# Probabilities transposed by a transfer of 16-bit halves, and a second layer two slices behind the first

## The chip, the core and the metric

The kernel runs on one core of a Trainium2 chip. A core has a matrix engine (TensorE, PE in the profile, with its weight loads as PEld), a vector engine (VectorE, DVE), a scalar engine (ScalarE, ACT), GpSimd (POOL) and SyncE (SP), which here only issues transfers. Each engine works through its own queue in order, and semaphores tie the queues together. Sixteen DMA engines move data between the chip's main memory (HBM) and the on-chip memory (SBUF), and within SBUF. TensorE writes to PSUM, eight banks of 128 x 512 floats.

The metric is the device time of one execution in microseconds: the median of three runs of the kernel before is 1006.57 us (1006.5 to 1007.86).

## The reference

Attention with a sliding window, with a few global tokens, followed by a dense two-layer network. Cut to what matters:

```python
# B = H = 8, Sl = 512 local and Sg = 32 global tokens, D = 64, window = 32
k_all, v_all = concat([k_g, k_l]), concat([v_g, v_l])
out_g = softmax(scale * q_g @ k_all.T) @ v_all
s_ll  = where(|i - j| <= window, scale * q_l @ k_l.T, -1e9)
out_l = softmax(concat([scale * q_l @ k_g.T, s_ll])) @ concat([v_g, v_l])
x = concat([out_g, out_l]) as [4608 tokens, 512]
h = x @ w_in                      # 512 -> 2048
out = (h * sigmoid(h)) @ w_out    # 2048 -> 512, float32
```

## The kernel before

**Attention in steps.** The local attention is cut into 64 steps (`steps`, numbered k): one step is a batch entry, a block of 128 queries and four of the eight heads. A step has two units i = 0, 1, and a unit has two heads u = 0, 1. For one head 128 queries meet W = 224 keys (128 + 2 x 32 local ones and 32 global ones). A step goes through these stages:

- `st_load`, `st_vload`: SP issues the loads of queries and keys (`raw`) and of values (`vraw`).
- `st_scores` (L352): 8 score products into the two PSUM banks "s".
- `st_soft`: per unit, `st_max` (L364, DVE: mask, scale and row minimum into the buffer `probs`), `st_exp` (L375, ACT), `st_norm` (L381, L383, DVE) and `st_scale` (ACT at L391 for u = 0, DVE at L389 for u = 1). There are two buffers `probs`, one for each unit.
- `st_move` (L397): SP copies the finished probabilities, 128 x 512 floats, from SBUF to SBUF into a buffer `rr` of the type float32r.
- `st_turn` (L427): TensorE turns them, four 128 x 128 transposes for each unit, into the "s" banks.
- `st_turned` (L439 on DVE, L441 on ACT): a copy from PSUM into `pt`, of which there are four.
- `st_with` (L453 to L456): POOL adds the global queries' columns to `pt`.
- `st_values` (L469): 16 products of `pt` with the values, into bank "x".
- `st_x` (L482 on ACT, L486 on DVE): the result as an upper part `xh` and a remainder `xl`, which are the network's input.

**Network in slices.** The tokens are cut into 12 blocks n of 2 or 3 tiles of 128 tokens, the hidden layer into 16 slices f of 128. Each float32 product is made of three float32r products (upper x upper, remainder x upper, upper x remainder). `first_layer(n, f)` is 12 products at L635 into one of two PSUM banks "h", then `g_tanh` (L642, ACT), `g_silu` (L646, DVE), `g_upper` (L652, ACT: `gh`) and `g_lower` (L658, DVE: `gl`). `second_layer(n, f)` is 9 products at L665 to L667. Before, the second layer runs one slice behind the first (`pend`). There are two buffers `gh` and one `gl`.

**What sets the order.** The start of the program, up to step 8 and the first block of tokens, is written out word by word (`START`). After that, the loop over blocks and slices hands out the stages of attention between the slices' products: each stage has a place on a scale of "step times" (`put`, `at(k)`, two units from one step to the next), and `fill` and `advance` release it when the share of the block's products that is done has come so far. In `group(k)` stand, for TensorE in this order, the transposes of step k - 1 (`turns`), the values of step k - 2 and the scores of step k. TensorE's order is the program's order; the order of the other engines is made by the scheduler of the compiler's tile layer, except where a dependency pins it. Loads have offsets of their own (`LOADS`). Global queries have their own chain (`g_scores` to `g_turned`), which the change leaves as it is.

Of the kernel before, what the change touches and what calls it, by code (L numbers as in the profile page):

```python
# [13 lines left out]
U32 = mybir.dt.uint32  # L14
AF = mybir.ActivationFunctionType
# [26 lines left out]
PARTS = 6  # L42
QK = P + W
# [37 lines left out]

FIRST = 0.6
APART, EARLY = 6, 0.1
LOADS = dict(load=-2.6, vload=0.3)
# [6 lines left out]
def attention_moe_kernel(ctx: ExitStack, tc: tile.TileContext, qk0_in, qk_in, v_in, gqk, wts, out):  # L91
# [33 lines left out]
    id32 = work.tile([P, P], F32R, tag="rr", bufs=2, name="id32").bitcast(F32)  # L125
# [30 lines left out]
    for t in probs:  # L156
        nc.gpsimd.memset(t[:, :, W:], 0.0)
    pgs = [const.tile([P, SKV], F32, name=f"pg{i}") for i in range(2)]
# [73 lines left out]
    def did(what, *needs):  # L232
        for need in needs:
            assert need in order_done, (what, need)
        order_done.add(what)

# [74 lines left out]
    def st_load(k):  # L311
        n = min(2, ND - 2 * k)
        of = qk0_in[2 * k : 2 * k + n].rearrange("i p n -> p i n")
        if k < WHOLE:

            if k % 4 < 2:
                raw = two.tile([P, 2 * (QW + W)], F32, tag="xh", name=f"raw{k}")
            else:
                raw = scratch(7 - k, F32, f"raw{k}")[:, : 2 * (QW + W)]
            nc.sync.dma_start(out=raw.rearrange("p (i n) -> p i n", i=2), in_=of)  # L320
            tiles["raw", k] = raw
            return
# [12 lines left out]
        tiles["raw", k] = raw  # L335
# [58 lines left out]
    def st_move(k, i):  # L394
        n = 2 * k + i
        rr = work.tile([P, 4 * P], F32R, tag="rr", bufs=2, name=f"rr{n}")
        nc.sync.dma_start(out=rr.bitcast(F32), in_=tiles["p", n])  # L397
# [12 lines left out]
    def st_turn(k, i):  # L410
# [11 lines left out]
        for m in range(4):  # L422
            sl = slice(m * P, (m + 1) * P)
            if k <= KF:
                nc.tensor.transpose(t[:, sl], p[:, sl], ident.bitcast(F32))  # L425
            else:
                nc.tensor.transpose(t[:, sl].bitcast(F32R), p[:, sl], ident)  # L427
# [44 lines left out]
    def st_x(k, rest=False):  # L472
# [8 lines left out]
        if not rest:  # L481
            nc.scalar.copy(out=xh[:, prs, sl], in_=src)  # L482
        if not rest and k >= AHEAD:
            return
        if rest:
            nc.vector.tensor_tensor(out=xl[:, prs, sl], in0=src, in1=xh[:, prs, sl].bitcast(F32), op=ALU.subtract)  # L486
            add_global(b, c, q2, gsrc)
        tiles.pop(("o", k))
# [70 lines left out]
    def put_last(n):  # L559

        places = [(two, "o", DM), (two, "o", DM), (raws, "vraw", DM // 2), (raws, "raw", DM // 2)]
        sb = [pool.tile([P, w], F32, tag=tag, name=f"o{n}_{i}") for i, (pool, tag, w) in enumerate(places)]
# [17 lines left out]
    plain_g = [two.tile([P, 3 * P], F32, tag="gh", name=f"g_first{t}") for t in range(2)]  # L580
# [57 lines left out]

    def g_tanh(n, f):
# [9 lines left out]
    def g_upper(n, f):  # L649
        nt = SIZES[n] * P  # L650
        gs[n, f] = [two.tile([P, 3 * P], F32R, tag="gh", name=f"gh{n}_{f}")]
        nc.scalar.copy(out=gs[n, f][0][:, :nt], in_=gs["t"][:, :nt])  # L652

    def g_lower(n, f):
        nt = SIZES[n] * P
        gs[n, f].append(two.tile([P, 3 * P], F32R, tag="gl", bufs=1, name=f"gl{n}_{f}"))
# [36 lines left out]
    traced, behind = nc.cur_bb.bb.instructions, {}  # L693
    pinned = mybir.DependencyInfo(mybir.DependencyClass.NoSync, mybir.DependencyReason.DATA)
# [25 lines left out]
    def turns(k):  # L720
        for i in range(2):
            st_turn(k, i)
        for i in range(2):
            st_turned(k, i)
            st_with(k, i)

    def group(k):

        if KF + APART < k <= len(steps):
            turns(k - 1)  # L730
        if k - 2 >= KF:
            st_values(k - 2)
            st_x(k - 2)
            st_x(k - 2, True)
        if k < len(steps):
# [15 lines left out]
    for k in range(KF + 1, len(steps) + 2):  # L751
        if k <= KF + APART:
# [35 lines left out]
    def fill(part):  # L788
# [3 lines left out]
        total = NF * SIZES[n] + (NF - 1) * SIZES[n] + SIZES[n - 1]  # L792
# [25 lines left out]
    pend = 0, PARTS - 1  # L818
    for n in range(1, len(SIZES)):
        for f in range(NF):  # L820
# [7 lines left out]
            second_layer(*pend)  # L828
            pend = n, f
    second_layer(*pend)  # L830
# [69 lines left out]
```

## Time and profile before

| what | value |
|---|---|
| median of the runs | 1006.57 us |
| the profiled execution | 1005.61 us |
| its span, first to last instruction | 1003.8 us |
| granted TensorE clock | 0.999 |
| L427 transposes | x440, in the trace from 108.6 to 905.0 us |
| L439 and L441, copies of the turned probabilities out of PSUM | 691 ns x63 and 583 ns x65 |
| POOL busy | 76.8 us, 8% of the span |
| moved by DMA | 110.15 MB, 110 GB/s mean |

A span is what lies between the first and the last instruction; the execution's own time is 1.8 us longer. Busy time of TensorE is no measure of its work by itself, because its products are pipelined and each is shown with its whole latency: consecutive products of 384 columns start 0.17 us apart and are each shown as 0.33 us long. What one costs is the distance from its start to the next one's.

### The profile page before, as it was taken

How to read it: one execution, taken by the hardware profiler on the slowest of the kernel's cores; microseconds unless marked ns; L12 is line 12 of the kernel's file. 1: busy time of each engine (PE TensorE's matmuls, PEld its weight loads, DVE VectorE, ACT ScalarE, POOL GpSimd, SP SyncE). 2: the span in 40 equal slices, each digit the busy share in tenths (PEclk: the TensorE clock that was granted, in tenths of full speed). 3: DMA queues.
4: the chain of work that ended last, by engine and by line, in shares of the span. 5: the costliest groups of instructions: out<-in, count | busy, mean ns of one | idle time of the engine just before them, and what ended most of it. 6: DMA issues, size and time to landing. Idle time of an engine off the chain costs nothing.

```text
span 1003.8 us, 17665 instructions
## 1 busy us (share of the span) xinstructions
PE 994.9 (99%) x6266; PEld 859.9 (86%) x6268; DVE 490.9 (49%) x1626; ACT 501.1 (50%) x1339; POOL 76.8 (8%) x234
## 2 busy tenths in 40 slices
PE   9999999999999999999999999999999999999998
PEld 5677887888888888888888888888888888888997
DVE  7887656444454445443445444544454444433222
ACT  7688676543554445453454444545444444432322
POOL 1033062000000000000000000000000000000000
PEclk9999999999999999999999999999999999999999
DMA  9973335322433224231142333324323231200001
GB/s 347 387 247 111 120 122 182 114 76 70 145 117 94 100 92 140 70 125 47 51 144 92 104 107 98 108 91 136 92 86 132 93 92 59 98 32 1 32 1 32
DMA packets 83880, 110.15 MB, mean 110 GB/s; under 512 B 7632, under 2 KB 55504, under 8 KB 83792
## 3 DMA queue, kind: packets, MB, share of 16 engines
q1 hardware_dynamic: 83456, 108.56, 32.8%
q8 instruction: 50, 0.82, 0.3%
q10 hardware_dynamic: 336, 0.46, 0.1%
q14 instruction: 38, 0.31, 0.1%
HBM read 67.37 MB, written 8.91 MB: 76 GB/s over the span
## 4 chain that ended last, share of the span: by engine, by line
PE 96%; DMA 1%; ACT 1%; DVE 1%; issue 1%; POOL 0%; POOLq 0%; ACTq 0%; DVEq 0%
PE h L635 36%; PE out L665 13%; PE out L666 12%; PE out L667 12%; PE o L469 7%; PE s L352 6%; PE t L427 3%; PE out L605 2%; PE gs L256 2%; PE h L589 2%; PE t L425 1%; PE gt L296 0%; PE idle L681 0%; DMA rr<-probs 0%; DMA raw<-in_qk_dram 0%
## 5 line engine op out<-in xcount | busy, mean ns | idle before, releaser
L635 PE MATMUL h<-xh,w_hi 128*128 128x384 f32 (+1 forms) x704 | 235.1, 334 | 0.0
L635 PE MATMUL h<-xh,w_lo 128*128 128x384 f32 (+1 forms) x704 | 233.9, 332 | 0.6 <-DMA w_lo<-w_lo 0.6
L635 PE MATMUL h<-xl,w_hi 128*128 128x384 f32 (+1 forms) x704 | 233.0, 331 | 0.0
L642 ACT ACTIVATE t<-h 128x384 f32<-128x384 f32 (+1 forms) x182 | 86.8, 477 | 272.9 <-PE h L635 271.0
L665 PE MATMUL out<-w_hi,gh 128*128 128x512 f32 x521 | 209.3, 402 | 0.0
L666 PE MATMUL out<-w_lo,gh 128*128 128x512 f32 x521 | 205.6, 395 | 0.0
L667 PE MATMUL out<-w_hi,gl 128*128 128x512 f32 x521 | 205.5, 394 | 0.0
L646 DVE SCALAR_TENSOR_TENSOR t<-t,h 128x384 f32<-128x384 f32 (+1 forms) x182 | 97.4, 535 | 209.9 <-ACT t L642 209.8
L658 DVE TENSOR_TENSOR gl<-t,gh 128x384 fp32r<-128x384 f32 (+1 forms) x182 | 100.1, 550 | 127.9 <-PE out L667 119.6
L635 PEld LDWEIGHTS h<-xh,w_hi 128*128 128x128 f32 x704 | 132.4, 188 | 10.6 <-issue 3.6
L635 PEld LDWEIGHTS h<-xl,w_hi 128*128 128x128 f32 x704 | 132.3, 188 | 6.7
L375 ACT ACTIVATE probs<-probs,st 128x224 f32<-128x224 f32 x236 | 111.5, 474 | 51.0 <-DVE st L364 51.0
L635 PEld LDWEIGHTS h<-xh,w_lo 128*128 128x128 f32 x704 | 132.2, 188 | 0.8 <-DMA w_lo<-w_lo 0.8
L652 ACT CAST gh<-t 128x384 fp32r<-128x384 f32 (+1 forms) x182 | 90.8, 499 | 76.4 <-DVE t L646 76.2
L665 PEld LDWEIGHTS out<-w_hi,gh 128*128 128x128 f32 x521 | 97.8, 188 | 29.7 <-issue 14.5
L667 PEld LDWEIGHTS out<-w_hi,gl 128*128 128x128 f32 x521 | 97.7, 188 | 21.9 <-DVE gl L658 0.5
L666 PEld LDWEIGHTS out<-w_lo,gh 128*128 128x128 f32 x521 | 97.9, 188 | 14.5
L453 POOL COPY pt<-pgt 128x64 f32<-128x64 f32 x120 | 29.5, 254 | 760.7 <-PE o L469 423.5
L364 DVE CUSTOM_DVE_ANT_0 probs<-s,mask 128x224 f32<-128x224 f32 x236 | 78.2, 387 | 4.8 <-PE s L352 4.8
L469 PE MATMUL o<-pt,vraw 128*64 128x160 f32 (+1 forms) x1024 | 78.2, 295 | 0.1
L439 DVE COPY pt<-t 128x512 f32<-128x512 f32 x63 | 43.4, 691 | 62.4 <-PE t L427 60.1
L469 PEld LDWEIGHTS o<-pt,vraw 128*64 128x64 f32 x1024 | 61.8, 136 | 6.5 <-issue 0.7
(104 smaller groups left out, 949.9 us busy)
## 6 DMA issues: line engine op xcount, KB each, us to landing
rr<-probs SPq DMA_DIRECT2D x110, 256.0 KB, 2.4
vraw<-in_v_dram SPq DMA_DIRECT2D x64, 256.0 KB, 2.7
raw_w<-in_wts_dram SPq DMA_DIRECT2D x32, 512.0 KB, 7.3
raw<-in_qk_dram SPq DMA_DIRECT2D x57, 224.0 KB, 2.8
graw<-in_gqk_dram SPq DMA_DIRECT2D x32, 304.0 KB, 3.3
out_dram<-o SPq DMA_DIRECT2D x30, 256.0 KB, 2.1
raw<-in_qk_dram SPq DMA_DIRECT2D x114, 64.0 KB, 2.4
pgr<-pg SPq DMA_DIRECT2D x12, 272.0 KB, 2.5
```

What stands on the lines that cost most here:

```text
L352: nc.tensor.matmul(s[u][:, i * W : (i + 1) * W], raw[rows, q : q + P], raw[rows, key : key + W], start=True, stop=True)
L364: nc.vector.tensor_tensor_reduce(out=p[:, u, :W], in0=s[u][:, i * W : (i + 1) * W], in1=mask_of[c], scale=-SCALE, scalar=3.0e38, op0=ALU.a ...
L375: nc.scalar.activation(p[:, u, :W], p[:, u, :W], AF.Exp, bias=st[:, m : m + 1], scale=-1.0, accum_out=st[:, 4 + m : 5 + m])
L469: nc.tensor.matmul(o[D * u : D * (u + 1), i * wide : i * wide + m], vraw[:, i, a, u, :], pts[i][:, u, a, :m], start=(a == 0), stop=(a == 1))
L635: nc.tensor.matmul(hs[n, f][:, :nt], wt, x, start=(i == 0), stop=(i == 3 * NCC - 1))
L642: nc.scalar.activation(t[:, :nt], hs[n, f][:, :nt], AF.Tanh, scale=0.5)
L646: nc.vector.scalar_tensor_tensor(out=t[:, :nt], in0=t[:, :nt], scalar=1.0, in1=hs.pop((n, f))[:, :nt], op0=ALU.add, op1=ALU.mult)
L652: nc.scalar.copy(out=gs[n, f][0][:, :nt], in_=gs["t"][:, :nt])
L658: nc.vector.tensor_tensor(out=gl[:, :nt], in0=gs["t"][:, :nt], in1=gh[:, :nt].bitcast(F32), op=ALU.subtract)
L665: nc.tensor.matmul(o, gh[:, sl], wh, start=(n > 0 and f == 0), stop=False)
L666: nc.tensor.matmul(o, gh[:, sl], wl, start=False, stop=False)
L667: nc.tensor.matmul(o, gl[:, sl], wh, start=False, stop=(f == (NF if n else PARTS) - 1))
```

## The change

From step 15 on (`TURNS = 15`) TensorE no longer transposes the local probabilities: 49 of the 64 steps. Instead:

- `st_split` (after's L408, DVE): the float32 words of a unit's probabilities are taken as pairs of 16-bit halves, and sorted into a plane of low halves and a plane of high halves (128 x 896 16-bit values, `planes`, one for each unit).
- L410: SP issues a transposing transfer of the planes, eight blocks of 128 x 128 16-bit values (256 KB), which lands in the buffer `probs` that the words came from.
- `st_join` (after's L417, ACT): a copy of 128 x 1024 16-bit values weaves the halves together again, into `pt`.

`st_move` goes for all steps; steps 9 to 14 are still turned by TensorE, straight from `probs` as float32. In `group(k)` the joins of step k - 1 now stand behind the values of step k - 2; `pt` has two buffers instead of four, and `raw` one instead of two from step 9 on, with its load asked for later. From the third block of tokens on (`LAG = 2`) the second layer runs two slices behind the first; `gh` and `gl` each have a ring of three places, made of buffers that are no longer used otherwise (`pt2`, `pt3`, `raw0`), and `g_upper` and `g_lower` are written out behind the second layer of the slice two before.

```diff
+LAG = 2
+
+TURNS = 15
...
-APART, EARLY = 6, 0.1
-LOADS = dict(load=-2.6, vload=0.3)
+EARLY = 0.1
+LOADS = dict(load=-1.9, vload=0.3)
...
+    planes = [const.tile([P, 2, 2, 2 * P], U16, name=f"planes{i}") for i in range(2)]
...
-        raw = raws.tile([P, 2 * QK], F32, tag="raw", name=f"raw{k}")
+        raw = raws.tile([P, 2 * QK], F32, tag=f"raw{k % 2 if k < KF else int(k > KF)}", bufs=1, name=f"raw{k}")
...
-    def st_move(k, i):
+
+    def st_split(k, i):
         n = 2 * k + i
-        rr = work.tile([P, 4 * P], F32R, tag="rr", bufs=2, name=f"rr{n}")
-        nc.sync.dma_start(out=rr.bitcast(F32), in_=tiles["p", n])
-        tiles["p", n] = rr
+        p = p_of(k, i)[:, :, :W].bitcast(U16).rearrange("p u (j h) -> p h u j", h=2)
+        nc.vector.tensor_copy(out=planes[i][:, :, :, :W], in_=p)
+        tiles["turned", n] = p_of(k, i).rearrange("p u j -> p (u j)").bitcast(U16).rearrange("p (g q) -> p g q", q=P)
+        nc.sync.dma_start_transpose(out=tiles["turned", n], in_=planes[i].rearrange("p h u j -> p (h u j)"))
+
+    def st_join(k, i):
+        _, b, c, q2 = steps[k]
+        n = 2 * k + i
+        did(("last", b, q2) if (c, i) == (NC - 1, 1) else ("step", n), ("turn", b, q2))
+        pt = pt_of(n).rearrange("p u a q -> p (u a) q").bitcast(U16)[:, :, : 2 * P].rearrange("p m (q h) -> p h m q", h=2)
+        nc.scalar.copy(out=pt, in_=tiles.pop(("turned", n)).rearrange("p (h m) q -> p h m q", h=2))
+        tc.add_manual_dep(traced[-1], state["evicted"], pinned, reason="join")
...
-            if k >= KF:
-                st_move(k, i)
+            if k >= TURNS:
+                st_split(k, i)
...
-            if k <= KF:
-                nc.tensor.transpose(t[:, sl], p[:, sl], ident.bitcast(F32))
-            else:
-                nc.tensor.transpose(t[:, sl].bitcast(F32R), p[:, sl], ident)
+            nc.tensor.transpose(t[:, sl], p[:, sl], ident.bitcast(F32))
...
-            tiles["pt", n] = work.tile([P, 2, 2, P + SG], F32, tag="pt", bufs=4, name=f"pt{n}")
+            tag = f"pt{n % (4 if n < 2 * TURNS else 2)}"
+            tiles["pt", n] = work.tile([P, 2, 2, P + SG], F32, tag=tag, name=f"pt{n}")
...
+    upper = [(two, "gh0"), (work, "pt2"), (two, "gh1")]
+    lower = [(work, "pt3"), (raws, "raw0"), (two, "gl")]
...
-        for i in range(2):
+        for i in range(2 if k < TURNS else 0):
             st_turn(k, i)
         for i in range(2):
-            st_turned(k, i)
+            (st_turned if k < TURNS else st_join)(k, i)
             st_with(k, i)
...
-        if KF + APART < k <= len(steps):
-            turns(k - 1)
         if k - 2 >= KF:
             st_values(k - 2)
             st_x(k - 2)
             st_x(k - 2, True)
+        if TURNS < k <= len(steps):
+            turns(k - 1)
...
-        for part in (g_tanh, g_silu, g_upper, g_lower):
+        for part in (g_tanh, g_silu) + (g_upper, g_lower) * (n < LAG):
             part(n, f)
...
-            second_layer(*pend)
-            pend = n, f
-    second_layer(*pend)
+            pend.append((n, f))
+            while len(pend) > (1 if n < LAG else 2):
+                second_layer(*pend.pop(0))
+            if n >= LAG:
+
+                for part, name in ((g_upper, "evicted"), (g_lower, "added")):
+                    part(n, f)
+                    if name in state:
+                        tc.add_manual_dep(traced[-1], state.pop(name), pinned, reason=name)
+    for slice_ in pend:
+        second_layer(*slice_)
```

How this stands in the queues is shown at the group of step 32, in block n = 4 of the tokens. TensorE's queue before: the last product of the slice h4_12, then the transposes of step 31 out of `rr`, the values of step 30 (`o30`), the scores of step 32 and the second layer of slice 11.

```order
L635 MATMUL h4_12_4678<-xh_4_3211,w_lo12_1860 128x384
L427 MATMUL t31_0_4698<-ident_88,rr62_4590 128x128 x4
L427 MATMUL t31_1_4699<-ident_88,rr63_4600 128x128 x4
L469 MATMUL o30_4718<-pt60_4545,vraw30_4468 64x160 x4
L469 MATMUL o30_4718<-pt61_4550,vraw30_4468 64x160 x4
L352 MATMUL s32_0_4730<-raw32_4525 128x224
L352 MATMUL s32_1_4731<-raw32_4525 128x224
L352 MATMUL s32_0_4730<-raw32_4525 128x224
L352 MATMUL s32_1_4731<-raw32_4525 128x224
L665 MATMUL out4_0_4086<-w_hi11_1819,gh4_11_4661 128x512
```

The same place in TensorE's queue with the change (all line numbers are after's):

```order
L656 MATMUL h4_12_4485<-xh_4_3086,w_lo12_1844 128x384
L487 MATMUL o30_4501<-pt60_4360,vraw30_4285 64x160 x4
L487 MATMUL o30_4501<-pt61_4365,vraw30_4285 64x160 x4
L362 MATMUL s32_0_4523<-raw32_4408 128x224
L362 MATMUL s32_1_4524<-raw32_4408 128x224
L362 MATMUL s32_0_4523<-raw32_4408 128x224
L362 MATMUL s32_1_4524<-raw32_4408 128x224
L694 MATMUL out4_0_4011<-w_hi10_1769,gh4_10_4452 128x512
```

The eight transposes are gone, the rest keeps its order, and the second layer that follows is that of slice 10 where it was that of slice 11.

ACT's queue at the same place before: tanh and upper part of slice 12 (`t4_12`, `gh4_12`) around the copy of a turned unit, the eviction `xh` of step 30, the exponentials and the scalings of step 32, tanh of slice 13.

```order
L642 ACTIVATE t4_12_4691<-h4_12_4678 128x384
L441 COPY pt62_4708<-t31_0_4698 128x4x128
L652 CAST gh4_12_4694<-t4_12_4691 128x384
L482 CAST xh_5_4123<-o30_4718 128x2x128
L375 ACTIVATE probs0_116,st32_4736<-probs0_116,st32_4736 128x224
L375 ACTIVATE probs1_117,st32_4736<-probs1_117,st32_4736 128x224
L375 ACTIVATE probs0_116,st32_4736<-probs0_116,st32_4736 128x224
L375 ACTIVATE probs1_117,st32_4736<-probs1_117,st32_4736 128x224
L391 ACTIVATE probs0_116<-probs0_116,st32_4736 128x224
L391 ACTIVATE probs1_117<-probs1_117,st32_4736 128x224
L642 ACTIVATE t4_13_4783<-h4_13_4770 128x384
```

With the change:

```order
L671 ACTIVATE t4_12_4498<-h4_12_4485 128x384
L500 CAST xh_5_3938<-o30_4501 128x2x128
L417 COPY pt62_4513<-probs0_116 128x2x4x128
L417 COPY pt63_4518<-probs1_117 128x2x4x128
L681 CAST gh4_12_4567<-t4_12_4498 128x384
L385 ACTIVATE probs0_116,st32_4529<-probs0_116,st32_4529 128x224 x2
L385 ACTIVATE probs1_117,st32_4529<-probs1_117,st32_4529 128x224 x2
L401 ACTIVATE probs0_116<-probs0_116,st32_4529 128x224
L401 ACTIVATE probs1_117<-probs1_117,st32_4529 128x224
L671 ACTIVATE t4_13_4584<-h4_13_4571 128x384
```

Both joins of step 31 stand between the eviction of step 30 and everything that ACT does for step 32; the upper part of slice 12 has moved behind them. On DVE the two splits (L408) stand behind both scalings of the step and ahead of the `g_silu` of slice 13.

SP's queue around step 31 with the change: the loads of the next step's queries and keys (`raw32`) and a move of the global chain (`pgr`) stand ahead of the transfers of step 31, the values of step 32 behind them.

```order
L350 DMA vraw31_4441<-in_v_dram 128x2x256
L337 DMA raw32_4408<-in_qk0_dram 64x2x128 x2
L338 DMA raw32_4408<-in_qk0_dram 128x2x224
L293 DMA pgr4_0_4412<-pg0_130 128x544
L410 DMA_TRANSPOSE probs0_116<-planes0_126 128x8x128
L410 DMA_TRANSPOSE probs1_117<-planes1_127 128x8x128
L293 DMA pgr4_1_4553<-pg1_131 128x544
L350 DMA vraw32_4562<-in_v_dram 128x2x256
```

The two transfers stand where the two moves into `rr` (L397) stood; before, the load of step 33 (`raw33`) stood ahead of the moves of step 31, so the load has come one step nearer to its use.

More of the change, by code (lines that the diff above doesn't have):

```diff
@@ L14 @@
 U32 = mybir.dt.uint32
+U16 = mybir.dt.uint16
 AF = mybir.ActivationFunctionType
@@ L124, in attention_moe_kernel @@
     nc.vector.memset(acc, 0.0)
-    id32 = work.tile([P, P], F32R, tag="rr", bufs=2, name="id32").bitcast(F32)
+    id32 = work.tile([P, P], F32, tag="pt0", name="id32")
     make_identity(nc, id32)
@@ L157, in attention_moe_kernel @@
         nc.gpsimd.memset(t[:, :, W:], 0.0)
+    planes = [const.tile([P, 2, 2, 2 * P], U16, name=f"planes{i}") for i in range(2)]
+    for t in planes:
+        nc.gpsimd.memset(t[:, :, :, W:], 0)
     pgs = [const.tile([P, SKV], F32, name=f"pg{i}") for i in range(2)]
@@ L235, in did @@
         order_done.add(what)
+    traced = nc.cur_bb.bb.instructions
+    pinned = mybir.DependencyInfo(mybir.DependencyClass.NoSync, mybir.DependencyReason.DATA)
     state = {}
@@ L482, in st_x @@
             nc.scalar.copy(out=xh[:, prs, sl], in_=src)
+            state["evicted"] = traced[-1].name
         if not rest and k >= AHEAD:
@@ L487, in st_x @@
             add_global(b, c, q2, gsrc)
+            state["added"] = traced[-1].name
         tiles.pop(("o", k))
@@ L559, in put_last @@
     def put_last(n):
-        places = [(two, "o", DM), (two, "o", DM), (raws, "vraw", DM // 2), (raws, "raw", DM // 2)]
-        sb = [pool.tile([P, w], F32, tag=tag, name=f"o{n}_{i}") for i, (pool, tag, w) in enumerate(places)]
+        places = [(two, "o", DM), (two, "o", DM), (raws, "vraw", DM // 2), (raws, "raw1", DM // 2)]
+        sb = [pool.tile([P, w], F32, tag=tag, bufs=1 if tag == "raw1" else 2, name=f"o{n}_{i}")
+              for i, (pool, tag, w) in enumerate(places)]
         src = outs[n][:2] + [outs[n][2][:, : DM // 2], outs[n][2][:, DM // 2 :]]
@@ L579, in attention_moe_kernel @@
     plain_h, plain_t = {}, two.tile([P, 3 * P], F32, tag="t", bufs=1, name="t_first")
-    plain_g = [two.tile([P, 3 * P], F32, tag="gh", name=f"g_first{t}") for t in range(2)]
+    plain_g = [two.tile([P, 3 * P], F32, tag=f"gh{t}", bufs=1, name=f"g_first{t}") for t in range(2)]
     def one(t, f):
@@ L636, in layer_products, with place @@
                 i += 1
+    upper = [(two, "gh0"), (work, "pt2"), (two, "gh1")]
+    lower = [(work, "pt3"), (raws, "raw0"), (two, "gl")]
+    def place(ring, short, n, f, name):
+        pool, tag = ring[((n - LAG) * NF + f) % 3] if n >= LAG else short[f % len(short)]
+        return pool.tile([P, 3 * P], F32R, tag=tag, bufs=1, name=f"{name}{n}_{f}")
     def g_tanh(n, f):
@@ L650, in g_upper @@
         nt = SIZES[n] * P
-        gs[n, f] = [two.tile([P, 3 * P], F32R, tag="gh", name=f"gh{n}_{f}")]
+        gs[n, f] = [place(upper, upper[::2], n, f, "gh")]
         nc.scalar.copy(out=gs[n, f][0][:, :nt], in_=gs["t"][:, :nt])
@@ L655, in g_lower @@
         nt = SIZES[n] * P
-        gs[n, f].append(two.tile([P, 3 * P], F32R, tag="gl", bufs=1, name=f"gl{n}_{f}"))
+        gs[n, f].append(place(lower, lower[2:], n, f, "gl"))
         gh, gl = gs[n, f]
@@ L692, in attention_moe_kernel @@
             does[name + letter] = partial(does[name], engine=engine)
-    traced, behind = nc.cur_bb.bb.instructions, {}
-    pinned = mybir.DependencyInfo(mybir.DependencyClass.NoSync, mybir.DependencyReason.DATA)
+    behind = {}
     for word in START.split():
@@ L751, in attention_moe_kernel @@
     for k in range(KF + 1, len(steps) + 2):
-        if k <= KF + APART:
+        if k <= TURNS:
             put(at(k) - (EARLY if k > KF + 1 else 0.4), turns, k - 1)
@@ L791, in fill @@
         n = now[0]
-        total = NF * SIZES[n] + (NF - 1) * SIZES[n] + SIZES[n - 1]
+        now_, then = (1 if m < LAG else 2 for m in (n, n - 1))
+        total = (2 * NF - now_) * SIZES[n] + then * SIZES[n - 1]
         if n + 1 < len(SIZES):
@@ L816, in second_layer @@
             put_out(n)
-    pend = 0, PARTS - 1
+    pend = [(0, PARTS - 1)]
     for n in range(1, len(SIZES)):
```

## The prediction

> **What bounds the kernel now.** First the page: span, busy times, and the chain of work that ended last.
>
> ```profile
> span 1003.8 us, 17665 instructions
> ...
> PE 994.9 (99%) x6266; PEld 859.9 (86%) x6268; DVE 490.9 (49%) x1626; ACT 501.1 (50%) x1339; POOL 76.8 (8%) x234
> ...
> PE 96%; DMA 1%; ACT 1%; DVE 1%; issue 1%; POOL 0%; POOLq 0%; ACTq 0%; DVEq 0%
> ```
>
> TensorE is busy for 99% of the span and carries 96% of the chain. Since its products overlap, the busy time alone proves little, so the second view is the windows, for the stretch in which all steps from 9 on are turned:
>
> ```profile
> 120.00:910.00 790.00, 789.24 (x4985) 692.56 (x4984) 373.95 (x1276) 385.26 (x1041) 52.55 (x178) 1.00 0.31 99
> ```
>
> Of 790.00 us TensorE shows work in 789.24, at the full clock (1.00), while DVE has 374 and ACT 385. Nothing that TensorE waits for is left to win there: **the time is the sum of what TensorE is given to do**. So the third view is its timeline, where a piece of work costs the distance from its start to the start of what follows.
>
> ```profile
> 514.20 0.39 PE L667 MATMUL out<-w_hi,gl 128*128 128x512 f32 x1
> 514.42 0.79 PE L427 MATMUL t<-ident,rr 128*128 128x128 f32 x8
> 515.15 1.20 PE L469 MATMUL o<-pt,vraw 128*64 128x160 f32 x16
> 516.28 1.03 PE L352 MATMUL s<-raw 64*128 64x224 f32 x8
> ```
>
> At 514.42 the eight transposes of a step take the place at which the next product would have started (514.20 + 0.23), and the values start at 515.15. That is **0.73 us a step**, not the 0.79 us shown nor the 243 ns of a single one. The same distance at other places:
>
> ```profile
> 162.08 0.80 PE L427 MATMUL t<-ident,rr 128*128 128x128 f32 x8
> 162.81 1.20 PE L469 MATMUL o<-pt,vraw 128*64 128x160 f32 x16
> ...
> 177.23 0.80 PE L427 MATMUL t<-ident,rr 128*128 128x128 f32 x8
> 177.96 1.31 PE L469 MATMUL o<-pt,vraw 128*64 128x160 f32 x16
> ...
> 190.39 0.80 PE L427 MATMUL t<-ident,rr 128*128 128x128 f32 x8
> 191.12 1.31 PE L469 MATMUL o<-pt,vraw 128*64 128x160 f32 x16
> ```
>
> 0.73 each time. The last view of this part is that of the line, for the number of steps and their distance:
>
> ```profile
> L427 PE MATMUL t<-ident,rr x440: 222/247/283, 108.8 to 905.0; 128*128 128x128 f32 x147
> ```
>
> 440 transposes are 55 steps (9 to 63), spread over 796 us: one step in 14.7 us.
>
> **What leaves TensorE.** Steps 15 to 63, 49 of them, lose their eight transposes: 49 x 0.73 = **35.8 us**, all on the path, because TensorE has no gaps there that could swallow it. What follows the transposes, the values, then follows a product as the transposes did, so no change-over is added. Steps 9 to 14 keep theirs, but in float32. What that costs is shown by step 8:
>
> ```profile
> 98.37 1.04 PE L425 MATMUL t<-ident,probs 128*128 128x128 f32 x8
> 99.16 0.47 PE L665 MATMUL out<-w_hi,gh 128*128 128x512 f32 x1
> ```
>
> 0.79 us for eight (98.37 to 99.16) against 0.73: 6 x 0.06 = 0.4 us back. Sum on TensorE: -35.4 us.
>
> **What is added, and what hides it.** Two splits on DVE, two transfers on SP, two joins on ACT for each of 49 steps; one copy on DVE and one on ACT go. The trace shows neither operation, so I bound them by rows of copies.
>
> ```profile
> L439 DVE COPY pt<-t 128x512 f32<-128x512 f32 x63 | 43.4, 691 | 62.4 <-PE t L427 60.1 <-PE t L425 1.3 <-POOL pt L453 0.2
> L389 DVE TENSOR_SCALAR probs<-probs,st 128x224 f32<-128x224 f32 x116 | 39.4, 340 | 1.5
> L646 DVE SCALAR_TENSOR_TENSOR t<-t,h 128x384 f32<-128x384 f32 x160 | 88.2, 552 | 198.7 <-ACT t L642 198.7
> L441 ACT COPY pt<-t 128x512 f32<-128x512 f32 x65 | 37.9, 583 | 15.3 <-PE t L427 12.7 <-PE t L425 1.6
> L652 ACT CAST gh<-t 128x384 fp32r<-128x384 f32 x160 | 81.9, 512 | 72.6 <-DVE t L646 72.4
> L486 DVE TENSOR_TENSOR xl<-o,xh 128x256 fp32r<-128x256 f32 x60 | 25.5, 425 | 42.4 <-ACT xh L482 42.3
> L482 ACT CAST xh<-o 128x256 fp32r<-128x256 f32 x60 | 22.3, 371 | 37.7 <-PE o L469 37.7
> L555 ACT ACTIVATE o<-out 128x512 f32<-128x512 f32 x31 | 18.6, 599 | 12.9 <-DMA out_dram<-o 10.9 <-PE out L667 1.9
> L278 DVE TENSOR_SCALAR pg<-pg,gst 128x544 f32<-128x544 f32 x16 | 8.2, 512 | 0.6
> ```
>
> Join, 1024 elements on ACT: 256 to 512 columns cost 371 to 599 ns, 0.89 ns a column, so 599 + 512 x 0.89 = 1.05 us; twice that if writing every other half word is slow, 2.1 us. I take 1.1, nearest to the rows. Split, 896 elements on DVE: from SBUF 224 to 544 columns cost 340 to 512 ns, which gives 0.70 us; from PSUM 256 to 512 columns cost 425 to 691 ns, which gives 1.09 us. I take 1.09, since the words are read in steps. In a step ACT then gains 2 x 1.1 - 0.58 = 1.6 us and DVE 2 x 1.09 - 0.69 = 1.5 us. By the window above they are busy for 385 and 374 of 790 us, 7.2 and 7.0 us of a step of 14.7; with 8.8 and 8.5 of 14.0 both stay under two thirds. Their load is thus hidden by TensorE; what counts is **where in the step** it stands.
>
> The first cover is that of the transfer. One step's softmax before:
>
> ```profile
> 500.11 1.03 PE L352 MATMUL s<-raw 64*128 64x224 f32 x8
> ...
> 500.23 0.37 ACT L482 CAST xh<-o 128x256 fp32r<-128x256 f32 x1 [0.84 <-PE o L469]
> ...
> 501.17 0.39 DVE L364 CUSTOM_DVE_ANT_0 probs<-s,mask 128x224 f32<-128x224 f32 x1
> ...
> 501.60 0.48 ACT L375 ACTIVATE probs<-probs,st 128x224 f32<-128x224 f32 x1 [1.01 <-DVE st L364]
> ...
> 503.02 0.47 ACT L375 ACTIVATE probs<-probs,st 128x224 f32<-128x224 f32 x1
> 503.61 1.06 ACT L391 ACTIVATE probs<-probs,st 128x224 f32<-128x224 f32 x2
> ...
> 504.12 1.21 SPq L397 DMA_DIRECT2D rr<-probs  x2
> ```
>
> `xh` ends at 500.60. The joins of the step before now stand right behind it on ACT: to 501.7 and 502.8. The transfer's target is the buffer that the maxima write, so the first maximum waits for the first join (501.7 where it was 501.17). On ACT one `gh` (0.51) and four exponentials (1.89 from 501.60 to the end of the last) follow, to 505.2, then the scalings (1.06) to 506.2. DVE scales and splits behind them: the splits end at about 507.1 and 508.2, and there the transfers go out, 3 to 3.5 us later than the moves at 504.12. The next step's `xh` ends 14.0 us after this one, at 514.6, and the second join starts at 515.7. So **each transfer has 7.5 us** before anybody waits. What one takes is bounded by these rows:
>
> ```profile
> rr<-probs SPq DMA_DIRECT2D x110, 256.0 KB, 2.4
> ...
> raw_w<-in_wts_dram SPq DMA_DIRECT2D x32, 512.0 KB, 7.3
> ...
> raw<-in_qk_dram SPq DMA_DIRECT2D x57, 224.0 KB, 2.8
> ...
> raw<-in_qk_dram SPq DMA_DIRECT2D x4, 32.0 KB, 2.2
> ```
>
> From below 2.4 us, the move that it replaces: as many bytes, SBUF to SBUF, same queue. From above 7.3 us, the slowest row, twice the bytes from HBM. I take the nearest, 2.4, with room to 4: hidden. At 7.3 it would still fit into the mean step, though not into the shortest: the values at 177.96 and 191.12 are 13.16 us apart, 1.57 under the mean, so up to 1.4 us late; at about half a us on average 49 x 0.45 = 22 us would be given back, 993 us. If it is late, ACT stands at the join, and behind it the exponentials, `gh` and `tanh` of the next slices, and so DVE.
>
> The page "VectorE: DVE Perf Modes" of the Trainium skill, in its section "The three transpose paths", gives 390 ns for a 128x128 transpose of 16-bit data on TensorE and 1309 ns for one by the transfer, and advises TensorE where a result in PSUM will do. It speaks against this change. The trace disagrees with its first figure as a price: eight take 0.73 us here, 91 ns each. Eight blocks at 1309 ns would be 10.5 us for a transfer, 3.0 beyond its cover, and 49 x 3.0 = 147 us, which by that estimate ends at 1118 us.
>
> The second cover is that of the slices. The two views for it are the chain in order of time and the waits:
>
> ```profile
> 502.03 2.10 PE h L635 x12
> ...
> 506.21 2.10 PE h L635 x12
> ```
>
> ```profile
> DVE gl L658 <- PE out L667: 119.6, 122, 1.4
> ```
>
> A first layer takes 2.10 us, the nine products up to 506.21 then 2.08. From the start T of a step's values: scores end at T + 2.1, then the second layer of slice 10 (to 4.2), h13 (6.3), slice 11 (8.4), h14 (10.5), slice 12 (12.5), h15. h15 writes the bank that h13's `g_silu` frees, and that stands on DVE behind the splits: 508.2 is T + 9.2 here (T is 499.0, as the values take 1.13 and the scores start at 500.11 in this step, a distance that the rows at 515.15 and 516.28 show), and with its own 0.55 us it ends at T + 9.8, **2.7 us ahead**. Slice 12's `gh` and `gl` are ready at about T + 5.2 and needed at T + 10.5; with the old distance of one slice they would have been needed at T + 6.3, so the second slice of distance is 4.2 us of cover for the joins, and no gain by itself: DVE's 119.6 us of waiting to overwrite `gl` cost TensorE nothing in the window above.
>
> At no cost: the loads of `raw`, asked for as the scores of the step before end, and `vraw`, which on SP stand ahead of and behind the transfers, have a step or nearly one (the row above: 2.8 us needed); POOL's two copies per step follow the join and are needed a step later; the joins wait for the values of the step before, as `xh` ahead of them does.
>
> **Sum.** 1003.8 - 35.8 + 0.4 = 968.4 us of span, with the 1.8 us around it (1005.61 for the profiled execution) 970.2. The median of the runs is 1.0 us above that execution's time, so **971 us**.
>
> **The rivals.**
> - *The transfer outlasts its cover* (slower). Decides at TensorE's loss of 0.73 us a step, so from 8.2 us on from issue to landing, be it for one or because the two of a step share the engines. At 9 us every step is 1.5 us late: 49 x 1.5 - 35.4 = +38, **1045 us**. For it: nothing in the trace shows a turning transfer. Against: 2.4 us for the same bytes, and DMA engines busy for a third of the time.
> - *The transfer goes block by block* (slower). Eight blocks of 32 KB, each with the 2.2 us of the row of that size, are 17.6 us, 10.1 over: 49 x 10.1 = 495, **1465 us**. The page of the Trainium skill named above has the milder form of it.
> - *ACT's and DVE's queue is late* (faster, by less). With joins of 2.1 us the splits end 2 us later: of the 2.7 us ahead of h15 0.7 is left, and steps that also carry an output's evictions (0.6 us each) or the global chain lose it. At 25 such steps and 0.7 us TensorE gets 17 us of waits: **988 us**. For it: the new work stands ahead of `gh`, `tanh` and `silu`; against: 2.1 is the far bound.
> - *No difference*: lateness happens to eat 0.73 us a step, **1006 us**.
>
> **Chances.** Forecast 0.63 (966 to 978), late queue 0.17 (978 to 1002), no difference 0.03, outlasted cover 0.12, block by block 0.05. A measurement here tells about 0.2% (2 us) from no change. Faster 0.80, same 0.03, slower 0.17. The range takes in the first two, with the 22 us of a 7.3 us transfer: 964 to 1002.
>
> **What would show it.** Right: no transposes but 48 + 72 in the early steps; values that start 0.23 us after a product; the transfer's row under 7.5 us; hardly any wait of ACT's join for the DMA; TensorE's busy share as before. Wrong: TensorE waiting at the first product of a slice for DVE's `t`, at a second layer for `gh` or `gl`, or ACT's join waiting for the transfer by microseconds in each step; joins or splits well over 1.1 us.

## The result, and the profile after

The changed kernel takes **975.2 us** (median of four runs, 975.01 to 976.73); the kernel before, in four runs beside it, 1006.58 us. The ratio is 0.9689, with a 95% interval of 0.9672 to 0.9705. The profiled execution took 975.09 us, 1.8 us of it around the span, at a granted clock of 0.999.

First the page of the changed kernel: the span, the busy time of each engine, the packets, and the chain of work that ended last.

```profile
span 973.3 us, 16895 instructions
...
PE 964.3 (99%) x5876; PEld 822.3 (84%) x5876; DVE 521.7 (54%) x1675; ACT 578.0 (59%) x1388; POOL 77.3 (8%) x236
...
DMA packets 171524, 106.94 MB, mean 110 GB/s; under 512 B 109360, under 2 KB 157232, under 8 KB 171440
...
PE 92%; DMA 3%; DVE 2%; ACT 2%; issue 0%; SPq 0%; POOL 0%; ACTq 0%
```

The span is 30.5 us shorter (1003.8 - 973.3), and TensorE is still busy for 99% of it. The busy times of ACT and DVE have risen by 77 and 31 us, which the kernel does not pay for. The 3% of the chain on DMA lie at the start, with the loads of the weights (`raw_w`). Of packets under 512 bytes there were 7632 and are 109360, at the same mean rate.

The same stretch as before in the windows (sum of PE, PEld, DVE, ACT and POOL, then clock, DMA share and GB/s):

```profile
120.00:910.00 790.00, 789.46 (x4761) 682.55 (x4760) 415.23 (x1345) 473.23 (x1111) 52.92 (x178) 1.00 0.42 98
```

TensorE has no more gaps than it had (789.24 before), so no wait has taken the place of the transposes. DVE and ACT have gone from 374 and 385 us to 415 and 473, the DMA engines from 0.31 to 0.42.

The timeline of TensorE at the group of step 39, at nearly the same time as the group of step 38 of which the prediction shows the rows (start, length shown, operation):

```profile
513.23 0.40 PE L696 MATMUL out<-w_hi,gl 128*128 128x512 f32 x1
513.56 1.20 PE L487 MATMUL o<-pt,vraw 128*64 128x160 f32 x16
514.69 1.03 PE L362 MATMUL s<-raw 64*128 64x224 f32 x8
```

The values start 0.33 us after the last product of the second layer, not 0.23. Behind a first layer's product of 384 columns it is the same: 0.27 us (409.29 to 409.56) where the transposes of before started after 0.17. That is the detail on which the size of the gain hangs.

### The profile page after: what moved, and what is told of

It reads as the page before. It is cut to its first block, busy times and chain, and to the rows that moved or that the text cites. A ratio compares the mean times of both kernels' runs of the same rounds, so it can differ in the third digit from the quotient of the medians.

```text
span 973.3 us, 16895 instructions
## 1 busy us (share of the span) xinstructions
PE 964.3 (99%) x5876; PEld 822.3 (84%) x5876; DVE 521.7 (54%) x1675; ACT 578.0 (59%) x1388; POOL 77.3 (8%) x236
## 2 busy tenths in 40 slices
DMA packets 171524, 106.94 MB, mean 110 GB/s; under 512 B 109360, under 2 KB 157232, under 8 KB 171440
## 4 chain that ended last, share of the span: by engine, by line
PE 92%; DMA 3%; DVE 2%; ACT 2%; issue 0%; SPq 0%; POOL 0%; ACTq 0%
PE h L656 37%; PE out L694 13%; PE out L695 12%; PE out L696 12%; PE o L487 7%; PE s L362 6%; DMA raw_w<-in_wts_dram 3%; PE gs L266 1%; PE out L626 1%; PE t L444 1%; PE h L610 1%; ACT w_hi L221 0%; PE gt L306 0%; DVE w L203 0%; PE out L839 0%
## 5 line engine op out<-in xcount | busy, mean ns | idle before, releaser
L417 ACT COPY pt<-probs 128x1024 uint16<-128x1024 uint16 x98 | 125.4, 1349 | 0.0
L374 DVE CUSTOM_DVE_ANT_0 probs<-s,mask 128x224 f32<-128x224 f32 x236 | 82.1, 388 | 62.0 <-ACT pt L417 57.0
```

What stands on the lines that cost most here:

```text
L374: nc.vector.tensor_tensor_reduce(out=p[:, u, :W], in0=s[u][:, i * W : (i + 1) * W], in1=mask_of[c], scale=-SCALE, scalar=3.0e38, op0=ALU.a ...
L417: nc.scalar.copy(out=pt, in_=tiles.pop(("turned", n)).rearrange("p (h m) q -> p h m q", h=2))
```

## The experiments

All ratios are to the kernel before, run beside each; "against the change" is the difference from its ratio, 0.9689, times 1006.6 us, and by the intervals of both it is known to about 2 us. In the kernels with the second layer one slice behind (3 and 6), with three transfers (8) and with repeated joins (9), the scheduler also moved some of ACT's and DVE's instructions, so that a loss there is that of the edit together with the new order; in 1, 5 and 7 it moved hardly any.

**1. The transposes back, nothing else undone.** All of the new work stays; in each of the 49 groups TensorE again turns eight blocks, of data that nobody reads.

```diff
+        if TURNS < k <= len(steps):
+            d = banks_s(f"d{k}")
+            for m in range(8):
+                to = d[m // 4][:, m % 4 * P : (m % 4 + 1) * P]
+                nc.tensor.transpose(to.bitcast(F32R), ident, ident)
+            back("s", f"d{k}")
         if k - 2 >= KF:
             st_values(k - 2)
```

> The changed kernel with the eight float32r transposes of each of the 49 steps put back on TensorE, ahead of the values, unused (the identity is turned into the two score banks); the transferred and joined probabilities are still what the values use. Theory A: a step's transposes are worth 0.63 us of TensorE (eight starts 0.08 us apart); the other 0.10 us between their start and that of the values is a change-over to the values that stays when they go. Then this kernel loses 49 x 0.63 = 30.9 us: 975.2 -> 1006, the time of the kernel before. Rival B: the transposes are worth 0.73 us, as predicted, and the missing 4 to 5 us are waits that the new work on ACT and DVE brings. Then it loses 49 x 0.73 = 35.8 us: 1011.

Measured: 1007.1 us against 1007.01, ratio 0.9998 (0.9989 to 1.0007). The two kernels cannot be told apart, and rival B's 1011, a ratio of 1.004, lies outside the interval. So the whole gain, 0.0309 x 1006.6 = 31.1 us, is what TensorE no longer does, 0.63 us a step; the splits, transfers, joins and the second slice of distance together neither cost nor bring anything, to within 1 us. With the transposes a step is longer and gives them more cover; that they cost nothing without them either is what the window above shows, with TensorE at work in 789.46 of 790 us. The timeline of TensorE in this kernel, at the group of step 38:

```profile
514.46 0.40 PE L696 MATMUL out<-w_hi,gl 128*128 128x512 f32 x1
514.69 0.80 PE L761 MATMUL d<-ident 128*128 128x128 f32 x8
515.42 1.20 PE L487 MATMUL o<-pt,vraw 128*64 128x160 f32 x16
```

From product to transposes 0.23, from there to the values 0.73, together 0.96. Without the transposes the same way takes 0.33. The difference is 0.63, and 0.10 of the 0.73 belong to the change from a product of the form 128*128 to one of the form 128*64, whether transposes or a layer's products precede it. (The form is what the rows give as 128*128, 128*64 or 64*128.)

**2. Unused transposes at another place.** The same eight, between the values and the scores, so that they stand between products of two other forms.

```diff
             st_values(k - 2)
+            if TURNS < k <= len(steps):
+                d = banks_s(f"d{k}")
...
             st_x(k - 2)
             st_x(k - 2, True)
```

> The changed kernel with the eight unused float32r transposes of each of the 49 steps back on TensorE, but between the values and the scores instead of ahead of the values. Theory H: the 0.10 us belongs to a change of the form of the array (128*128 for products and transposes, 128*64 for the values, 64*128 for the scores), so transposes among full-array products cost 0.63 us, and between two other forms one change more, 0.73 us: 49 x 0.73 - 49 x 0.63 = +4.9 us against the transposes ahead of the values, ratio to before 1.0047, 1011.5. Against H (the gap belongs to the values alone, or to whatever comes after a 512-column product): no difference, ratio 1.000, 1007.

Measured: 1020.67 against 1007.14, ratio 1.0128 (1.0111 to 1.0145): 13 us more than in experiment 1 for the same instructions, 0.27 us a step. TensorE's timeline of this kernel:

```profile
520.36 1.20 PE L487 MATMUL o<-pt,vraw 128*64 128x160 f32 x16
521.49 0.89 PE L763 MATMUL d<-ident 128*128 128x128 f32 x8
522.30 1.15 PE L362 MATMUL s<-raw 64*128 64x224 f32 x8
523.38 1.14 PE L266 MATMUL gs<-graw 128*64 128x272 f32 x8
```

The values take 1.13 to the next start, as ever. The transposes take 0.81 instead of 0.73, and the scores 1.08 where they took 0.96 (a row of the chain below). That is 0.81 + 0.12 = 0.93 a step, against 0.63 among products of their own form; the 0.30 more and the 0.27 of the times agree within the intervals. By the single starts in the trace, the last transpose stands 0.18 us ahead of the first score, as it stood 0.18 ahead of the first value in experiment 1, while the transposes themselves start 0.08 to 0.09 apart: that is the 0.10 of one change of form more, as theory H has it. The other 0.20 are no change-over: 0.08 lies among the transposes, which start somewhat further apart than in experiment 1, and 0.12 among the scores. Why both are slower here stays open.

**3. The second layer one slice behind.** The transfers stay, the second slice of distance goes.

```diff
-LAG = 2
+LAG = 99
```

> The changed kernel with the second layer one slice behind the first throughout (LAG = 99), all else kept. Theory A: the second slice of distance is only cover for the joins. In the step at 499 us of the changed kernel's trace gl is done 0.8 us or more before the old distance would need it, so most steps lose nothing; steps with evictions of an output or the global chain lose some: 0 to +8 us, 975 to 983. Rival C: without it the joins ahead of gh and gl stop TensorE in nearly every step, by about 1 us: +40 to +50 us, 1015 to 1025, and the whole gain hangs on it.

Measured: 984.79, ratio 0.9773 (0.9757 to 0.9789), 8.5 us against the change. The distance is worth that much as cover, and no more. TensorE's waits for an output bank, none in the changed kernel, add up to 6.5 us here (3.9 for ACT's evictions, 2.6 for outputs' transfers). Where they arise shows in the timeline of this kernel at the end of a block of tokens:

```profile
583.72 2.64 SPq L410 DMA_TRANSPOSE probs<-planes  x2
...
586.42 4.27 SPq L577 DMA_DIRECT2D out_dram<-o  x6
...
589.71 0.60 ACT L575 ACTIVATE o<-out 128x512 f32<-128x512 f32 x1 [0.99 <-DMA out_dram<-o]
...
590.36 0.50 PE L694 MATMUL out<-w_hi,gh 128*128 128x512 f32 x1 [1.92 <-DMA out_dram<-o]
```

SP holds the two transposing transfers from 583.72 to 586.36 and only then issues the output's. ACT's eviction waits for a buffer that such a transfer empties, and the next block's product, which needs the bank, waits 1.92 us.

**4. The distance alone.** The kernel before, with the second layer two slices behind and the buffers that this takes, but with the transposes on TensorE. The buffers `gh` and `gl` are rings of two here, not of three.

```diff
+LAG = 2
...
-    second_layer(*pend)
+            pend.append((n, f))
+            while len(pend) > (1 if n < LAG else 2):
+                second_layer(*pend.pop(0))
...
```

> The kernel before with only the second layer two slices behind the first (from the third block on; two buffers for the upper and two for the lower parts, one of them taken from the second raw buffer, whose load is asked for later as in the change). Theory A: no gain of its own, TensorE had no waits to lose: 1006.6 within 1.5 us. Rival E: the distance pays by itself: 1000 to 1004.

Measured: 1007.41 against 1007.01, ratio 1.0001 (0.9992 to 1.0011). No gain of its own.

**5. The move without the turning.** The same bytes through the same queue by a plain transfer, so that the probabilities are not turned.

```diff
-        nc.sync.dma_start_transpose(out=tiles["turned", n], in_=planes[i].rearrange("p h u j -> p (h u j)"))
+        nc.sync.dma_start(out=tiles["turned", n].rearrange("p g q -> p (g q)"), in_=planes[i].rearrange("p h u j -> p (h u j)"))
```

> The changed kernel with a plain move of the planes into the same buffer in place of the transposing transfer: the same bytes and the same places in all queues, but nothing is turned, so the probabilities that the values meet are not transposed. What is measured is the price of turning itself. Theory F: landing 2.4 us as the old move had instead of 3.2, SP held for 0.6 us instead of 1.3, and no change in the time: 974 to 976. Rival: the crossbar's small packets or SP's longer hold cost TensorE something somewhere: 970 to 973.

Measured: 974.64, ratio 0.9682 (0.9667 to 0.9696), 0.7 us less than the change, which the intervals do not tell apart. The view of the buffer `probs`: first the changed kernel (count, then shortest, mean and longest hold of SP's queue in ns), then the plain move:

```profile
L410 SPq DMA_TRANSPOSE probs<-planes x98: 1231/1278/2354, 170.0 to 863.8; - x98
...
DMA to landing us min/median/max: 3.0/3.2/5.3
```

```profile
L410 SPq DMA_DIRECT2D probs<-planes x98: 465/519/1582, 169.7 to 862.6; - x98
...
DMA to landing us min/median/max: 2.2/2.4/4.4
```

Turning costs 0.8 us to the landing and 0.76 us of SP for each transfer, both hidden here.

**6. One slice behind, with the plain move.** Edits 3 and 5 together, to see how much of edit 3's loss is SP's hold.

> The one-slice distance (LAG = 99) together with the plain move in place of the transposing transfer (nothing is turned). With one slice the loss was 9 to 10 us, in TensorE's waits for the third output bank of a block: its eviction on ACT waits for an output's transfer, which SP issued behind two transposing transfers that hold it for 1.3 us each. If SP's hold is what makes that late, the plain move (0.5 us each) takes back at least half: 976 to 980. If it is the joins ahead of the evictions on ACT, the time stays: 982 to 985.

Measured: 978.58, ratio 0.9718 (0.9701 to 0.9734). Against experiment 5 the missing distance now costs 0.0036 x 1006.6 = 3.6 us where it cost 8.5. About half of the loss of experiment 3 (8.5 - 3.6 = 4.9 us, known to some 3 us) is thus the turning transfers' hold on SP's queue or their later landing, which this does not separate; the rest is there with a plain move too. TensorE's waits for the output bank fall likewise, from 6.5 to 2.1 us.

**7 and 8. The transfers twice, and three times.** Each unit's transfer is repeated (`range(2)` in 7, `range(3)` in 8), so that the last landing comes later. SP's queue and the DMA engines are held longer with it, so the two prices come together.

```diff
+        for _ in range(2):
+            nc.sync.dma_start_transpose(...)
```

> The changed kernel with each pair of transposing transfers issued twice; the second pair waits for the first and writes the same. In the changed kernel's trace a pair lands about 3.2 us before the joins want it (issue at 536.5, 3.2 us to landing, join at 542.9), so one more round of 3.2 us just fits. Theory F (a step is a ring: join, maximum, exponentials, split, transfer, join; TensorE loses only what the ring is longer than the step): -2 to +20 us against the change, 975 to 995. Rival G (the transfer is on the path already, or the DMA engines are the limit): +3.2 us in each of 49 steps, +150 us, 1130.

> The same with each pair issued three times: 6.4 us more in the ring, of which about 3.2 fit. Theory F: 2 to 3.2 us a step are late, +100 to +160 us, 1075 to 1135: this prices the rival in the prediction by which the transfer outlasts its cover. Against F: no loss (the cover is longer than the ring says) or +310 us (there was none).

Measured: 983.84, ratio 0.9769 (0.9755 to 0.9784), 8.1 us against the change; and 1105.72, ratio 1.0975 (1.0952 to 1.0998), 129.5 us against it. The waits of the kernel with three (engine, tile and line, who was waited for: us in total, times, longest):

```profile
ACT pt L418 <- DMA probs<-planes: 168.8, 49, 7.8
...
PE out L695 <- ACT o L576: 45.8, 8, 9.5
...
PE h L657 <- DVE t L676: 20.0, 8, 5.4
```

In the changed kernel no join waits for its transfer at all; with two they wait 26 times, for 38 us, with three 49 times. So two more transfers a step mostly fit and four do not: the first two cost 8 us, the next two 121. Its windows show one thing more, the clock:

```profile
200.00:900.00 700.00, 627.86 (x3571) 533.90 (x3569) 318.90 (x1045) 366.86 (x850) 26.45 (x124) 0.95 0.72 151
```

TensorE has 72 us of gaps here, and its granted clock averages 0.95, not 1.00.

**9. The joins twice.** Each join's copy is issued a second time: 2.7 us more of ACT in a step, ahead of `gh` and of the exponentials, and so of the splits and transfers too.

```diff
+        for _ in range(2):
+            nc.scalar.copy(out=pt, in_=src)
...
```

> The changed kernel with each join done twice: 2.7 us more for ACT in each step, in front of gh, the exponentials and tanh. It stands for the prediction's rival in which ACT's queue is late (joins of 2.1 us each, priced at 17 us; here they are 2.7). Theory F: the second unit's part of the ring gets 2.7 us longer, about 3.2 were free, so most steps still fit, and steps with evictions or the global chain don't: +10 to +50 us, 985 to 1025. Rival: hidden altogether, 975 to 978, as ACT is busy for 60% only.

Measured: 980.09, ratio 0.9732 (0.9716 to 0.9748), 4.3 us against the change. The joins of this kernel in the view of lines (count, busy us, mean ns, idle before):

```profile
L419 ACT COPY pt<-probs 128x1024 uint16<-128x1024 uint16 x196 | 253.2, 1351 | 4.4 <-DMA probs<-planes 4.2
```

Twice the joins, 128 us more on ACT, cost 4.3 us, outside both expectations: neither fully hidden nor the ten and more that a scarce cover would have cost. Of it 2.9 us are waits of TensorE, new in this kernel, of the global chain's transposes (`gt`) for DVE's `st`.

**10. Transfers from step 9 on.** Six more steps without transposes, in the dense start of the program.

```diff
-TURNS = 15
+TURNS = 9
```

> The changed kernel with the transfer from step 9 on instead of step 15 (TURNS = 9): six more steps. Theory A (TensorE's sum of work rules there too): float32 transposes cost about 0.69 us a step net of the change-over, 6 x 0.69 = 4.1 us less: 971. Rival D: in the stretch up to 170 us ACT and DVE still split weights and the second layer is one slice behind until the third block, so joins and splits are late and TensorE waits: 975 to 985.

Measured: 982.32, ratio 0.9751 (0.9737 to 0.9766), 6.2 us worse than the change instead of some 4 better. Its waits:

```profile
PE out L694 <- ACT gh L681: 5.2, 4, 2.1
...
PE out L696 <- DVE gl L687: 1.8, 3, 1.2
```

These lie where the second layer still runs one slice behind and steps are short: there the joins delay `gh` and `gl`, and TensorE waits for them. The granted clock is lower there too, 0.91 from 120 to 140 us and 0.96 from 140 to 170, where it is 1.00 in the changed kernel.

**11. The same, with two slices from the second block on.** If that wait were all, this version would beat the change.

```diff
-LAG = 2
+LAG = 1
-TURNS = 15
+TURNS = 9
```

> The transfer from step 9 on and the two-slice distance one block earlier (TURNS = 9, LAG = 1). With TURNS = 9 alone TensorE waited for gh and gl at the second layer at 130, 141, 153, 164 and 166 us, all while the distance was one slice. If the short distance is the whole cause, these 7 us go and six steps of transposes are saved: 970 to 972, better than the change. Rival: steps there are only 11 to 12 us apart, shorter than ring plus weight splitting, so ACT's joins wait for the transfer and TensorE for g_silu: 976 to 982.

Measured: 983.74, ratio 0.9762 (0.9746 to 0.9778), 7.3 us against the change. The waits for `gh` and `gl` are gone, and others have come:

```profile
ACT pt L417 <- DMA probs<-planes: 6.4, 5, 3.0
...
PE gs L266 <- DVE acc L517: 3.4, 1, 3.4
...
PE h L656 <- DMA w_lo<-w_lo: 2.6, 1, 2.6
```

The windows of that stretch, first the changed kernel and then this one:

```profile
140.00:170.00 30.00, 29.46 (x221) 24.48 (x220) 20.14 (x71) 21.25 (x62) 13.94 (x18) 1.00 0.36 110
```

```profile
140.00:170.00 30.00, 23.75 (x143) 18.70 (x142) 18.77 (x58) 22.23 (x55) 14.06 (x14) 0.87 0.60 132
```

TensorE loses 5.7 us in 30, at a clock of 0.87, while POOL and DVE are still splitting weights and the transfers take DMA time. Which of these would have to move first was not tried. Neither of the two versions beats the change.

## Why the prediction was right, and where it was off

**What bounds the kernel** was right: the time is the sum of what TensorE is given. Experiment 1 shows it as directly as can be, since giving the transposes back gives the old time back.

**The saving on TensorE** was the mis-sized term. The prediction had 49 x 0.73 = 35.8 us, less 0.4 for the steps that turn in float32, so 968.4 us of span; the span is 973.3. The step that failed reads "What follows the transposes, the values, then follows a product as the transposes did, so no change-over is added". It is true that the transposes followed a product in 0.23 us. But the values do not: they need 0.33, as the timelines show. The start-to-start distance of 0.73 had that change of form in it, and it stayed behind when the transposes went. The sum with the true price is 49 x 0.63 - 0.4 = 30.5 us, the difference of the two profiled spans. That it meets it to a tenth is luck: four runs of the kernel before lie 1.4 us apart, the medians differ by 31.4, and the 0.4 was too small as well. It was read at step 8, whose transposes are followed by a product. In the changed kernel eight float32 transposes take 0.97 us where the values follow, against 0.73 in float32r:

```profile
149.39 1.03 PE L444 MATMUL t<-ident,probs 128*128 128x128 f32 x8
150.36 1.20 PE L487 MATMUL o<-pt,vraw 128*64 128x160 f32 x16
```

The price of 0.63 was in the profile of before, in the chain in order of time (start, length, operation and count), a view of which the prediction quoted other rows; the row of the same step reads:

```profile
514.59 0.63 PE t L427 x8
```

And the chain of the changed kernel there:

```profile
513.39 0.23 PE out L696
513.63 1.13 PE o L487 x16
514.76 0.96 PE s L362 x8
```

A piece of the chain runs from one end to the next, so 0.63 is what disappears, and the values keep their 1.13. (The ends of products are modelled in the profile; that 0.63 is the price is shown by experiment 1.) The weight loads show the change of form too:

```profile
513.00 0.19 PEld L696 LDWEIGHTS out<-w_hi,gl 128*128 128x128 f32 x1
...
513.55 0.96 PEld L487 LDWEIGHTS o<-pt,vraw 128*64 128x64 f32 x16 [0.37 <-issue]
```

The load for the product at 513.23 starts 0.23 us ahead of it, during the product before; the first load for the values, at 513.56, starts only 0.01 us ahead. The view of waits has this idle time of the weight loads 54 times, and had it twice, for 0.7 us, before:

```profile
PEld o L487 <- issue: 16.8, 54, 0.4
```

The Trainium skill has the rule that the prediction should have weighed: "TensorEngine Tiling (Array Packing)", section "Key Properties", says that changing the tiling mode drains TensorE. It gives no figure; the trace agrees in kind, with 0.33 against 0.23 us at this place and with the 0.10 ahead of the scores in experiment 2; whether draining is what takes this time no run here shows.

**Split and join** were sized from neighbouring rows. In the lines of the changed kernel:

```profile
L417 ACT COPY pt<-probs 128x1024 uint16<-128x1024 uint16 x98 | 125.4, 1349 | 0.0
...
L408 DVE COPY planes<-probs 128x896 uint16<-128x896 uint16 x98 | 58.8, 622 | 0.3
```

The join takes 1.35 us, not 1.1, between the bounds of 1.05 and 2.1. The split takes 0.62, not 1.09, and less than the lower bound of 0.70: the rows of copies with 32-bit elements did not bound a copy of 16-bit ones. With TensorE at work in 789.46 of 790 us, neither is on the path.

**The transfer** took 3.2 us where 2.4 with room to 4 was taken. Its cover in a short step, by the timeline of ACT, DVE and SP of the changed kernel (length of x2 groups is that of both):

```profile
530.13 0.37 ACT L500 CAST xh<-o 128x256 fp32r<-128x256 f32 x1 [0.76 <-PE o L487]
...
530.40 2.55 ACT L417 COPY pt<-probs 128x1024 uint16<-128x1024 uint16 x2
...
531.78 0.39 DVE L374 CUSTOM_DVE_ANT_0 probs<-s,mask 128x224 f32<-128x224 f32 x1 [0.69 <-ACT pt L417]
...
535.10 1.07 ACT L401 ACTIVATE probs<-probs,st 128x224 f32<-128x224 f32 x2
...
535.88 1.16 DVE L408 COPY planes<-probs 128x896 uint16<-128x896 uint16 x2
...
536.52 2.64 SPq L410 DMA_TRANSPOSE probs<-planes  x2
...
542.92 2.57 ACT L417 COPY pt<-probs 128x1024 uint16<-128x1024 uint16 x2
```

The joins hold up the first maximum by 0.69 us, where the prediction's times gave 0.5 (501.17 to 501.7); from the end of `xh` (530.50) to the transfers are 6.0 us, against 6.5 in the prediction's working (500.60 to 507.1). The landing of the two, in the view of the line for this step:

```profile
DMA to landing us min/median/max: 3.4/3.7/3.9
```

The first takes the 3.9 us, so it lands at 540.4 and is wanted at 542.92: 2.5 us to spare in a step of only 12.5 us. (The expectation of experiment 7 took the median of 3.2 and had 3.2 to spare.) In the tightest steps of the trace 1.3 us are left: the transfer issued at 758.3 lands 5.3 us later, and its join starts at 765.0. So that the transfer stayed hidden owes something to luck, since the prediction had given each 7.5 us of cover; by how little it holds, experiments 7 and 8 show.

**The distance of two slices** was "cover for the joins, and no gain by itself": right, by experiments 3 and 4. What it covers is 8.5 us, and about half of that comes not with the joins but with the turning transfers, which hold SP's queue at the ends of the blocks (experiment 6); the prediction had not seen this. Its working of this cover read the order of the step at 499 us wrongly: three products of the second layer, not nine, stand there between the scores and the next first layer, which by its own row starts at 502.03, T + 3.0 and not T + 4.2. The first layer that it calls h15 then starts at about T + 11.4, and `g_silu`, which ends at T + 9.8 in the prediction's working, is 1.6 us ahead of it, not 2.7. It was enough: TensorE never waits for DVE's `t` at a first layer in the changed kernel.

**The rivals.** *The transfer outlasts its cover* did not happen, but its mechanism is real: in experiment 8 each repetition waits for the landing of the same unit's transfer before it, so the last transfer of a step is issued 8.0 us behind the first and lands 11.0 us after it (508.83, 516.79 and 519.87 in one step). The prediction priced 9 us at 1045; its formula gives 49 x (11.0 - 7.5) - 35.4 = 136 us more than before for 11.0, 1143 us. Measured were 1105.7. In that kernel TensorE's waits are 45.8 us for output banks and 20.0 us at first layers, at a clock of 0.95; how much each of them adds was not separated. *Block by block* is excluded by the landing at 3.2 us. *The late queue* was priced at 17 us for joins of 2.1 us; experiment 9, with 2.7 us for each pair of copies, cost 4.3. In the changed kernel TensorE waits for `gh` once, for 0.3 us, and DVE's wait to overwrite `gl` has shrunk from 119.6 us to 2.2:

```profile
DVE gl L687 <- PE out L696: 2.2, 4, 0.7
```

## What to carry to other kernels

On an engine without gaps, price a removed instruction by its piece in the chain of waits, or by the distance between its two neighbours with and without it, never by its own start-to-start distance: this holds the successor's change of array form, which stays. Work moved off such an engine earns its full price only while its ring (here join, maximum, exponential, scaling, split, transfer, next join) closes within the step; two more transfers a step cost 8 us and four cost 130, so measure the spare time before filling it. A longer software pipeline is cover, worth nothing alone (1.0001) and 8.5 us under the new work.

## What the runs showed of the hardware that was not expected

- The price of an instruction on TensorE depends on the array forms of both neighbours: the change from 128*128 to 128*64 costs 0.10 us, and eight transposes of the full array cost 0.63 us a step among products of their own form but 0.90 (by the times) to 0.93 (by the timeline) between the values (128*64) and the scores (64*128).
- A transposing transfer of 256 KB of 16-bit values is nearly as fast as a plain one, 3.2 us to landing against 2.4, but it holds SP's queue for 1.28 us instead of 0.52, and what is queued behind it can feel that: with one slice of distance 8.5 us were lost with turning transfers and 3.6 with plain ones.
- The split, 896 16-bit values read at a step of four bytes, takes DVE 0.62 us; the join, 1024 written at such a step, takes ACT 1.35 us.
- The granted clock averaged 0.95 and 0.87 in the stretches in which TensorE had gaps (experiments 8 and 11), and 1.00 in the same stretches of the changed kernel, without them.
